# Attention and a feed-forward block in one kernel: one weight tile's sums kept in SBUF, and the order of GpSimd's work around them

## The chip, the cores and the metric

The kernel runs on one NeuronCore of a Trainium2 chip. The metric is the device time in microseconds of one execution, taken from the first to the last instruction with what lies around them; lower is better. The engines are named as the profile names them: PE (TensorE, matmuls; PEld are its weight loads), DVE (VectorE), ACT (ScalarE), POOL (GpSimd) and SP (SyncE, which issues the DMAs here).

## The reference

Masked attention over 8 batches, 8 heads, 576 positions and a head size of 64 (half of the heads look at a window of 32 positions, half at every 32nd position), and behind it a feed-forward block of 512 to 2048 to 512 over all 4608 tokens:

```python
scores = scale * np.matmul(q, k.transpose(0, 1, 3, 2))
scores = np.where(masks[None, :, :, :], scores, -1000000000.0)
scores = scores - np.max(scores, axis=-1, keepdims=True)
attn = np.exp(scores)
attn = attn / (np.sum(attn, axis=-1, keepdims=True) + 1e-09)
x = np.matmul(attn, v)          # heads side by side: 4608 x 512
h = x @ w_in                    # 512 x 2048
g = h * (1.0 / (1.0 + np.exp(-1.702 * h)))
out = g @ w_out                 # 2048 x 512
```

## The kernel before

Attention is worked in pairs (48 of them, six per batch, alternately of the windowed kind "l" with tiles of 96 rows and of the strided kind "s" with 128 rows). One pair passes through these steps: `scores` (PE, into the two banks `s_banks`), `masked` and `maxima` (DVE), `below` (subtract the maximum, GpSimd, but on DVE for pair 6, lines 301 to 304), `exps` (ACT), `totals` (DVE), `scaled` (GpSimd, line 323), `turn` (PE transposes, then an ACT copy `kept`), `values` (PE, again into `s_banks`) and the copies `moved` (ACT), which put the result into the four blocks x11, x12, x21, x22 of a batch's x.

The product with `w_in` is done batch by batch, over eight weight tiles (`FP` = 8). Every operand is split into a high part (a cast on ACT: `w_high`, `t_high`, `x_high`) and a low part (a subtraction on DVE: `w_low_part`, `t_low`, `x_low`), and three matmuls (high by high, high by low of x, low of w by high) stand for one. From the second batch on, and for tiles 6 and 7 of the first, the product of a weight tile is formed with seven block products instead of eight (`product(n, k)` and `combine(n, k)`, n counts tiles through all batches). These need sums and differences of the four blocks of x (`x_sum`, `first_sums`: s1 = x21 + x22, s2, s3 = x11 - x21, which is made in the place of x21, s4 = x12 - s2) and of the four blocks of each weight tile (`t_sum`, four GpSimd subtractions of 128x256, then `t_high` and `t_low` into kinds 3 to 6 of the tile). For tiles 0 to 5 of the first batch the eight plain block products are used (`plain(n, u)`, "units" of six matmuls), since their sums aren't there yet.

Where a tile's sums come from: the words of weight tile i arrive in a buffer `raw_i` and are decoded there by ACT and DVE (`w_scale`, `w_low`, `w_join`). For tiles in `DIRECT` (line 439: 0, 6 and 7) the sums are formed in that buffer, which then stays in use until `t_low`. The others are written to a DRAM tile (`w_store`, 512 KB) and read back later (`t_load`) into the shared tile `sums`, three at a time. Raw buffers, weight tiles `w_i`, `sums` and two early inputs rotate in nine buffers of the same size (`wp`, line 136).

The order of the work is written out by hand. The first pairs and the first unit are in `OPENING` (line 695). Then comes one slot after the other: a slot s issues one unit or product on PE, and behind it what `side(s, ...)` registered for it, in the order of registration (`sided`, line 1018). Slots 8 to 50 hold the units and the first products of tiles 6 and 7, pass 1 (batch 1, products n = 8 on) begins at slot 59 (`HEAD`). Every engine's instructions and every DMA issue stay in this program order (class `InOrder`, line 80), so an instruction that waits holds all that stands behind it on its engine. The slots of pairs 6 to 11 are set in lines 767 to 777, those of the raw words in 782 to 790, of the tiles' sums in 791 to 804, of the first batch's sums and differences in 805 to 809, and of later batches' x sums in 753 to 764.

Of the kernel before, what the change touches and what calls it, by code (L numbers as in the profile page):

```python
# [15 lines left out]
ALU = mybir.AluOpType  # L16
# [14 lines left out]
FP = DFF // (2 * P)  # L31
PAIRS = 6
# [10 lines left out]
PLAIN = 6  # L43
SEVEN = 8 * PLAIN - 3
# [28 lines left out]
def attn_ffn(ctx, tc, qk, vs, weights, masks, ident, out):  # L73
# [6 lines left out]
    class InOrder:  # L80
# [16 lines left out]
    vector, scalar, gpsimd, sync = (  # L97
        InOrder(e, strict) for e in (nc.vector, nc.scalar, nc.gpsimd, nc.sync)
    )
# [64 lines left out]
    for j in (1, 2, 3, 0, 4, 5):  # L164
# [3 lines left out]
        t = prs[j].rearrange("p (i m) -> p i m", i=4)  # L168
# [76 lines left out]
    def parts_of(p, banks, at=0):  # L245

        nq, nk, _, mask = geom(p)
        pr = pr_of(p).rearrange("p (i m) -> p i m", i=4)[:, :, 1 : 1 + 2 * WL]
        pr = pr.rearrange("p i (j n) -> p i j n", j=2)
        heads = pr[:nq, :, :, :nk]  # L250
        srcs = banks and [
            bank[:nq, at : at + 4 * WL].rearrange("p (i n) -> p i n", i=4)[:, :, :nk]
            for bank in banks
        ]
        if p not in sums_of:
            sums_of[p] = [
                small.tile([P, 8], F32, tag=x, name=f"{x}_{p}") for x in ("nmax", "ssum", "rinv")
            ]
        return nq, nk, mask, pr, heads, srcs, sums_of[p]
# [4 lines left out]
    def each(t, nk):  # L264
        t = t.rearrange("p (i j) -> p i j", j=2)
        return t.unsqueeze(3).broadcast_to([t.shape[0], 4, 2, nk])
# [33 lines left out]

    def below(p, banks):
        nq, nk, _, _, heads, _, (nmax, _, _) = parts_of(p, banks)
        engine = vector if p == PAIRS else gpsimd
        engine.tensor_tensor(out=heads, in0=heads, in1=each(nmax[:nq], nk), op=ALU.add)

    def exps(p, banks):
# [60 lines left out]
    def moves_of(moves):  # L367
        for u in range(U):
            for move in moves:
                move(u)  # L370
# [22 lines left out]
    def x_from(k, b):  # L393
        if b is None and k in (1, 6):
            return apart[(PLAIN + (k == 6)) % 2]
        names = {0: "11", 2: "12", 5: "22", 6: "21"} if b == 0 else ("11", "11", "12", "s3", "s1", "22", "12")
        return halves[names[k]]
# [12 lines left out]
    def x_sum(k, b):  # L410
        x11, x12, x21, x22, s1 = (halves[x] for x in ("11", "12", "21", "22", "s1"))
        s2 = x_from(1, b)
        if k == 1:
            vector.tensor_tensor(out=s1, in0=x21, in1=x22, op=ALU.add)
        elif k == 2:
            vector.tensor_tensor(out=s2, in0=x22, in1=x21, op=ALU.subtract)
        elif k == 3:
            (vector if b == 1 else gpsimd).tensor_tensor(
                out=x21, in0=x11, in1=x21, op=ALU.subtract
            )  # L420
        else:
            (vector if b == 1 else gpsimd).tensor_tensor(
                out=x12, in0=x12, in1=s2, op=ALU.subtract
            )


    def first_sums(*which):

        x11, x12, x21, x22 = (halves[x] for x in ("11", "12", "21", "22"))
        s2, s3, s1, s4 = (x_from(k, None) for k in (1, 3, 4, 6))  # L430
        for k in which:
            o, x, y, op = {
                1: (s2, x22, s3, ALU.subtract), 6: (s4, x12, s2, ALU.subtract),
                4: (s1, x21, x22, ALU.add), 3: (s3, x11, x21, ALU.subtract),
            }[k]
            gpsimd.tensor_tensor(out=o, in0=x, in1=y, op=op)

    KINDS = (0, 5, 1, 6, 3, 4, 2)
    DIRECT = (0, *range(PLAIN, FP))

    def w_words(which, i, raw):

# [37 lines left out]
    def w_store(i):  # L480
        if i not in DIRECT:
            sync.dma_start(out=plains[i].rearrange("p (q n) -> p q n", q=4), in_=words[i])
# [8 lines left out]
    def t_view(i):  # L491

        if i in DIRECT:
            return spent[i].rearrange("p (q n) -> p q n", q=4)
        if "sums" not in made:
            made["sums"] = wp.tile([P, WLEN], F32, tag="w", name="sums", bufs=FP + 1)
        k = i % 3
        return made["sums"][:, k * 1024 : (k + 1) * 1024].rearrange("p (q n) -> p q n", q=4)
# [4 lines left out]
    def t_sum(i, m):  # L503

        b11, b21, b22, b12 = ((words[i] if i in DIRECT else t_view(i))[:, q] for q in range(4))
        t3, t4, t5, t6 = (t_view(i)[:, q] for q in range(4))
# [209 lines left out]
    def side(s, f, *a):  # L716
        sides.setdefault(s, []).append((f, a))

    def first(b):
        return HEAD + PASS * (b - 1) if b else 0  # L720
# [16 lines left out]
    def groups_of(b, slots):  # L737

        for g in range(3):
            q, s, then = b * PAIRS + 2 * g, slots[g] + 3 * (g > 0), slots[g + 1]  # L740
            side(s, both_scores, q)
            for i in range(2):
                s += 2 * i * (g == 0)
                side(s + i, masked, q + i, s_banks, 256 * i)
                for f, d in (
                    (maxima, 0), (below, 0), (exps, 4), (totals, 5),
                    (scaled, 5 + (i and g > 0)),
                ):
                    side(s + d + i, f, q + i, s_banks)
                side(then - (3 - (g > 0), 1)[i], turn, q + i, s_banks[i])  # L750
            side(then, both_values, q)

    for b in range(B):
        at = first(b)
        if b:
            c = {1: -2, 2: 1}.get(b, 0)
            side(at - 10 - c, x_sum, 1, b)
            side(at - 9 - c, x_sum, 3, b)
            for k in range(7):
                t = at + 2 * k - 6 + (k == 1)  # L760
                side(t, x_high, k, b)
                side(t + 1, x_low, k, b)
            side(at - 4, x_sum, 2, b)
            side(at, x_sum, 4, b)
        if 1 < b < B - 1:
            groups_of(b + 1, [at + t for t in (3, 16, 30, 44)])
        for i in range(PAIRS if b < 2 else 0):
            p = (b + 1) * PAIRS + i
            s = at - 3 * b + 7 * i + 2 * (not b)
            t = ((4, 5, 6, 11, 12) if b else (2, 3, 3, 11, 13)) if not i else (4, 5, 5, 10, 12) if i == PAIRS - 1 and not b else (5, 6, 7, 10, 12)  # L770
            side(s, scores, p, s_banks)
            side(s, load_qk, p + 2)
            for f, d in ((masked, 0), (maxima, 1), (below, 2), (exps, t[0]), (totals, t[1]), (scaled, t[2])):
                side(s + d, f, p, s_banks)
            side(s + t[3], turn, p, s_banks[0])
            side(s + t[4], lambda p=p: moves_of([values(p, s_banks)]))
            side(s + t[4], load_v, p + 2)
# [4 lines left out]
    for i in range(2, FP):  # L782
        at = 7 * (i - 2) + 6
# [6 lines left out]
            side(at + t, f, i)  # L790
    for i in range(FP):
        if i in DIRECT:
            at = 7 * (i - 2) + 6
            for m in range(4):
                side(at + 4 + m // 2 if i else 9, t_sum, i, m)
            for t, f in ((8, t_high), (9, t_low)) if i else ((16, t_high), (17, t_low)):
                side(at + t if i else t, f, i)
            continue
        load = -8 + i if i < 4 else 7 * i - 20
        sums, high, low = (1, 5, 6) if i == 1 else (7 * i - 10 + t for t in (0, 6, 8))  # L800
        for m in range(4):
            side(HEAD + sums + (2 if i > 1 and m > 1 else 0), t_sum, i, m)
        for t, f in ((load, t_load), (high, t_high), (low, t_low)):
            side(HEAD + t, f, i)
    side(1, first_sums, 4, 3)
    side(5, first_sums, 1, 6)
    for t, k in ((18, 3), (24, 1), (31, 4), (SEVEN + 2, 6)):
        side(t, x_high, k, None)
        side(t + 1, x_low, k, None)

# [70 lines left out]
    for h in range(12):  # L881
        at = last + STEP * (h // 2) + 16 + 3 * (h % 2)
# [126 lines left out]
    for i, n in enumerate((0, 1, 2, 3)):  # L1009
        at = last + (15, 23, 31, 45)[i]  # L1010
# [14 lines left out]
    for s in range(8, first(B)):  # L1025
        if s in units:
            plain(*divmod(units[s], 8))
        else:
            at = s - HEAD + PASS
            for n in (at // STEP, at // STEP - 1):  # L1030
                k, odd = divmod(at - STEP * n, 2)
# [151 lines left out]
```

## Time and profile before

| | us |
|---|---|
| three runs, median (lowest, highest) | 847.0 (846.14, 847.84) |
| the profiled execution, its own time | 847.13 |
| its span, first to last instruction | 845.3 |
| PE busy | 822.4 |
| DVE busy | 607.2 |
| POOL busy | 507.3 |
| ACT busy | 418.1 |

The span is the time in which instructions run; the time of an execution has some 1.8 us more around it. Busy times count an engine's own instructions without its waits. The mean granted clock of PE in this execution was 0.986 of full speed.

### The profile page before, as it was taken

The page shows a single profiled execution, that of the slowest core. Times are in us where ns is not written, and L with a number is a line of the kernel's source. Part 1 is how long each engine was busy: PE and PEld are TensorE (multiplying, and loading weights), DVE is VectorE, ACT ScalarE, POOL GpSimd, SP SyncE. Part 2 cuts the span into 40 slices and gives each one's busy share as a digit, 9 for nine tenths or more (in the row PEclk, how much of TensorE's full clock was granted, in tenths as well). Part 3 has the DMA queues.
Part 4 walks back from the last instruction along what each step waited for, and adds up shares of the span by engine and source line. Part 5 has one row for each costly group of instructions (what it writes and reads, how often), then busy time and mean ns, then how long its engine had stood idle before and what let it go on. Part 6 is the DMA issues. An engine that isn't in the chain of part 4 may idle for free.

```text
span 845.3 us, 22494 instructions
## 1 busy us (share of the span) xinstructions
PE 822.4 (97%) x9020; PEld 768.5 (91%) x9025; DVE 607.2 (72%) x1026; ACT 418.1 (49%) x646; POOL 507.3 (60%) x511
## 2 busy tenths in 40 slices
PE   7978989999999999999999999999999999999998
PEld 5868979999999999999999999889889889888898
DVE  5756777676866777768567886888777667677774
ACT  4657533343443444444346565555555555555550
POOL 4644276144333333433335539999999999999990
PEclk9979989999999999999999999999999999999999
DMA  9787556476676685766757974444444444444431
GB/s 344 287 304 249 180 163 206 147 240 222 209 240 229 204 275 183 249 226 203 245 190 258 299 244 129 147 125 131 141 129 134 153 145 144 127 146 128 125 100 50
DMA packets 111640, 161.59 MB, mean 191 GB/s; under 512 B 9648, under 2 KB 88240, under 8 KB 110640
## 3 DMA queue, kind: packets, MB, share of 16 engines
q1 hardware_dynamic: 111536, 160.16, 58.3%
q8 instruction: 71, 1.16, 0.6%
q14 instruction: 33, 0.27, 0.1%
HBM read 102.97 MB, written 57.15 MB: 189 GB/s over the span
## 4 chain that ended last, share of the span: by engine, by line
PE 86%; DVE 0%; issue 0%
PE my L89 27%; PE mx L89 23%; PE mz L89 21%; PE s L89 15%; DVE w L89 0%; DVE arena L89 0%; DVE nmax L89 0%
## 5 line engine op out<-in xcount | busy, mean ns | idle before, releaser
L89 POOL TENSOR_TENSOR arena<-arena 128x256 f32<-128x256 f32 (+1 forms) x302 | 342.9, 1151 | 119.8 <-ACT arena L89 44.8
L89 DVE TENSOR_TENSOR xa<-arena,xa 128x576 fp32r<-128x576 f32 (+3 forms) x116 | 158.8, 1371 | 38.5 <-ACT xa L89 37.5
L89 PE MATMUL my<-xa,w 128*128 128x288 f32 x1128 | 180.8, 302 | 2.5 <-DVE w L89 2.5
L89 ACT CAST xa<-arena 128x576 fp32r<-128x576 f32 (+3 forms) x107 | 118.0, 1122 | 99.7 <-PE s L89 24.4
L89 PEld LDWEIGHTS my<-xa,w 128*128 128x128 f32 x1128 | 157.0, 189 | 5.3 <-DVE w L89 2.7
L89 DVE TENSOR_TENSOR arena<-my,arena 128x288 f32<-128x288 f32 (+1 forms) x230 | 100.3, 442 | 63.2 <-PE my L89 60.7
L89 ACT COPY arena<-mx 128x288 f32<-128x288 f32 (+3 forms) x167 | 57.6, 366 | 171.9 <-PE mx L89 112.0
L89 PE MATMUL mx<-xa,w 128*128 128x288 f32 x804 | 133.5, 304 | 3.8 <-ACT arena L89 3.8
L89 PE MATMUL mz<-xa,w 128*128 128x288 f32 x792 | 129.2, 299 | 0.5 <-DVE xa L89 0.5
L89 ACT ACTIVATE arena<-arena 128x1024 f32<-128x1024 f32 (+2 forms) x120 | 105.1, 876 | 36.3 <-POOL arena L89 20.9
L89 POOL TENSOR_TENSOR arena<-arena,nmax 96x512 f32<-96x512 f32 (+1 forms) x41 | 52.7, 1286 | 115.9 <-DVE nmax L89 108.3
L89 PEld LDWEIGHTS mx<-xa,w 128*128 128x128 f32 x804 | 116.6, 194 | 4.9 <-ACT arena L89 4.0
L89 PEld LDWEIGHTS mz<-xa,w 128*128 128x128 f32 x792 | 112.1, 189 | 1.4 <-DVE xa L89 0.7
L89 DVE TENSOR_TENSOR arena<-mz,arena 128x288 f32<-128x288 f32 (+1 forms) x172 | 75.2, 440 | 31.7 <-PE mz L89 27.6
L89 POOL TENSOR_TENSOR arena<-arena,rinv 96x512 f32<-96x512 f32 (+1 forms) x48 | 47.0, 988 | 54.9 <-DVE rinv L89 38.8
L89 PE MATMUL mx<-w_out,xa 128*128 128x512 f32 (+1 forms) x378 | 72.3, 317 | 0.0
L89 PE MATMUL mz<-w_out,xa 128*128 128x512 f32 (+1 forms) x366 | 71.4, 320 | 0.0
L89 PE MATMUL my<-w_out,xa 128*128 128x512 f32 (+1 forms) x366 | 71.3, 320 | 0.0
L89 DVE TENSOR_TENSOR ga<-arena,ga 128x1792 fp32r<-128x1792 f32 (+1 forms) x31 | 56.6, 1824 | 16.1 <-ACT ga L89 16.1
L89 PE MATMUL s<-w_out,xa 128*128 128x512 f32 (+1 forms) x378 | 67.8, 321 | 0.0
L89 ACT CAST ga<-arena 128x1792 fp32r<-128x1792 f32 (+1 forms) x25 | 40.8, 1632 | 46.6 <-PE s L89 10.4
L89 PEld LDWEIGHTS s<-w_out,xa 128*128 128x128 f32 x378 | 54.9, 188 | 5.8
(83 smaller groups left out, 1094.7 us busy)
## 6 DMA issues: line engine op xcount, KB each, us to landing
hid<-arena SPq DMA_DIRECT2D x256, 144.0 KB, 3.4
arena<-hid SPq DMA_DIRECT2D x144, 256.0 KB, 3.3
arena<-qk SPq DMA_DIRECT2D x23, 448.0 KB, 4.9
arena<-qk SPq DMA_DIRECT2D x21, 472.0 KB, 5.6
arena<-vs SPq DMA_DIRECT2D x23, 384.0 KB, 4.8
out<-arena SPq DMA_DIRECT2D x34, 256.0 KB, 3.9
stage<-w_out SPq DMA_DIRECT2D x16, 512.0 KB, 4.3
raw<-w_in SPq DMA_DIRECT2D x7, 1024.0 KB, 7.9
```

The lines of the kernel that those rows point to most:

```text
L89: ins = call(*args, **kw)
```

## The change

`below` of pair 7 goes from GpSimd to VectorE, like that of pair 6. Pair 6's transposes and value products come one slot earlier. For batch 1, `x_sum` 3 and 4 go from VectorE to GpSimd, where they are for all other batches. In `first_sums`, s2 is formed as s1 - x11 instead of x22 - s3 (the same value), so the order becomes s1, s2, s4, s3. Tile 1 joins `DIRECT`: its store and its load fall away, its sums are formed in its raw buffer in slots 19 and 20 (before: in slot 60), its casts are in slots 24 and 25 (before: 64 and 65). The casts of difference 1 of the first batch go from slots 24 and 25 to 27 and 28. Tile 0's casts, and sums and casts of tiles 6 and 7, come one slot later (38, 39, 42, 43 become 39, 40, 43, 44; 45, 46, 49, 50 become 46, 47, 50, 51). The loads of tiles 2 and 3 come one slot earlier.

```diff
@@ below
-        engine = vector if p == PAIRS else gpsimd
+        engine = vector if PAIRS <= p < PAIRS + 2 else gpsimd
@@ x_sum
-            (vector if b == 1 else gpsimd).tensor_tensor(
+            gpsimd.tensor_tensor(
                 out=x21, in0=x11, in1=x21, op=ALU.subtract
             )
         else:
-            (vector if b == 1 else gpsimd).tensor_tensor(
+            gpsimd.tensor_tensor(
                 out=x12, in0=x12, in1=s2, op=ALU.subtract
             )
@@ first_sums
-                1: (s2, x22, s3, ALU.subtract), 6: (s4, x12, s2, ALU.subtract),
+                1: (s2, s1, x11, ALU.subtract), 6: (s4, x12, s2, ALU.subtract),
@@
-    DIRECT = (0, *range(PLAIN, FP))
+    DIRECT = (0, 1, *range(PLAIN, FP))
@@ slots of pair 6: exps, totals, scaled, turn, values
-            t = ((4, 5, 6, 11, 12) if b else (2, 3, 3, 11, 13)) if not i else ...
+            t = ((4, 5, 6, 11, 12) if b else (2, 3, 3, 10, 12)) if not i else ...
@@
         if i in DIRECT:
-            at = 7 * (i - 2) + 6
+            at = 7 * (i - 2) + 11
+            places = ((9, 9, 17, 18), (19, 20, 24, 25))[i] if i < 2 else (at, at + 1, at + 4, at + 5)
             for m in range(4):
-                side(at + 4 + m // 2 if i else 9, t_sum, i, m)
-            for t, f in ((8, t_high), (9, t_low)) if i else ((16, t_high), (17, t_low)):
-                side(at + t if i else t, f, i)
+                side(places[m // 2], t_sum, i, m)
+            side(places[2], t_high, i)
+            side(places[3], t_low, i)
             continue
-        load = -8 + i if i < 4 else 7 * i - 20
-        sums, high, low = (1, 5, 6) if i == 1 else (7 * i - 10 + t for t in (0, 6, 8))
+        load = -9 + i if i < 4 else 7 * i - 20
+        sums, high, low = (7 * i - 10 + t for t in (0, 6, 8))
@@
-    side(1, first_sums, 4, 3)
-    side(5, first_sums, 1, 6)
-    for t, k in ((18, 3), (24, 1), (31, 4), (SEVEN + 2, 6)):
+    side(1, first_sums, 4, 1)
+    side(5, first_sums, 6, 3)
+    for t, k in ((18, 3), (27, 1), (31, 4), (SEVEN + 2, 6)):
```

## Rows read from the trace of the kernel before

**Rows 1.** The page, part 1: busy time, share of the span, instructions by engine
```profile
PE 822.4 (97%) x9020; PEld 768.5 (91%) x9025; DVE 607.2 (72%) x1026; ACT 418.1 (49%) x646; POOL 507.3 (60%) x511
```

**Rows 2.** Waits of PE from 30 us on: total us, times, longest us
```profile
PE s L89 <- ACT arena L89: 6.6, 2, 6.2
PE mx L89 <- ACT arena L89: 3.8, 1, 3.8
PE my L89 <- DVE w L89: 2.5, 1, 2.5
```

**Rows 3.** Windows: stretch, length, busy us by engine, granted clock, DMA share, GB/s
```profile
49.30:54.90 5.60, 5.60 (x51) 5.48 (x52) 3.45 (x5) 2.13 (x5) 2.39 (x2) 0.53 0.69 235
54.90:81.80 26.90, 26.89 (x449) 25.10 (x447) 20.12 (x32) 19.11 (x34) 9.76 (x11) 1.00 0.82 278
...
85.60:88.70 3.10, 3.10 (x13) 3.10 (x14) 2.04 (x2) 0.00 (x0) 0.93 (x2) 0.50 0.14 48
...
113.50:119.40 5.90, 5.90 (x64) 5.24 (x68) 2.66 (x6) 2.49 (x7) 3.26 (x4) 0.50 0.55 183
```

**Rows 4.** Timeline, POOL: start us, us, instruction, [idle before <-releaser]
```profile
34.22 3.18 POOL L89 TENSOR_TENSOR arena<-arena 128x576 f32<-128x576 f32 x2
37.77 0.92 POOL L89 TENSOR_TENSOR arena<-arena,rinv 128x432 f32<-128x432 f32 x1 [0.37 <-DVE rinv L89]
38.64 4.78 POOL L89 TENSOR_TENSOR arena<-arena 128x576 f32<-128x576 f32 x2
43.38 2.89 POOL L89 TENSOR_TENSOR raw<-raw 128x256 f32<-128x256 f32 x4
46.23 1.04 POOL L89 TENSOR_TENSOR arena<-arena,nmax 96x512 f32<-96x512 f32 x1
```

**Rows 5.** Timeline, ACT then PE, around the first wait
```profile
42.29 0.40 ACT L89 COPY arena<-mx 128x288 f32<-128x288 f32 x1
47.30 0.63 ACT L89 ACTIVATE arena<-arena 96x512 f32<-96x512 f32 x1 [4.61 <-POOL arena L89]
...
48.84 0.68 ACT L89 COPY arena<-s 128x108 f32<-128x108 f32 x4
...
49.27 1.41 PE L89 MATMUL s<-arena 64*64 64x54 f32 x32 [6.21 <-ACT arena L89]
...
54.86 0.49 PE L89 MATMUL s<-ident_sb,arena 96*128 96x96 f32 x4
```

**Rows 6.** Timeline, DVE: `below` of pair 6, tile 2's low part
```profile
34.73 1.37 DVE L89 TENSOR_TENSOR arena<-arena,nmax 128x432 f32<-128x432 f32 x1
...
40.88 1.27 DVE L89 TENSOR_TENSOR w<-raw,w 128x1024 fp32r<-128x1024 f32 x1 [0.16 <-ACT w L89]
```

**Rows 7.** Timeline, DVE, POOL and ACT, ahead of the second wait
```profile
77.50 0.67 DVE L89 TENSOR_REDUCE nmax<-arena 96x8 f32<-96x512 f32 x1
...
79.04 1.75 POOL L89 TENSOR_TENSOR arena<-arena,nmax 96x512 f32<-96x512 f32 x1
...
80.83 0.63 ACT L89 ACTIVATE arena<-arena 96x512 f32<-96x512 f32 x1 [1.59 <-POOL arena L89]
...
84.17 1.07 ACT L89 CAST w<-raw 128x1024 fp32r<-128x1024 f32 x1
85.11 0.43 ACT L89 COPY arena<-mx 128x288 f32<-128x288 f32 x1
```

**Rows 8.** Timeline, POOL, PE and DVE, around the third wait
```profile
103.36 4.47 POOL L89 TENSOR_TENSOR sums<-sums 128x256 f32<-128x256 f32 x4
...
109.37 0.93 PE L89 MATMUL mz<-xa,w 128*128 128x288 f32 x5 [0.47 <-DVE xa L89]
...
112.21 1.21 DVE L89 TENSOR_TENSOR w<-sums,w 128x1024 fp32r<-128x1024 f32 x1
```

**Rows 9.** Timeline, ACT and PE: tile 7's cast, products 7.1 and 6.5
```profile
93.64 1.06 ACT L89 CAST w<-raw 128x1024 fp32r<-128x1024 f32 x1
...
96.38 1.74 PE L89 MATMUL my<-xa,w 128*128 128x288 f32 x12
```

More of the change, by code (lines that the diff above doesn't have):

```diff
@@ L769, in attn_ffn @@
             s = at - 3 * b + 7 * i + 2 * (not b)
-            t = ((4, 5, 6, 11, 12) if b else (2, 3, 3, 11, 13)) if not i else (4, 5, 5, 10, 12) if i == PAIRS - 1 and not b else (5, 6, 7, 10, 12)
+            t = ((4, 5, 6, 11, 12) if b else (2, 3, 3, 10, 12)) if not i else (4, 5, 5, 10, 12) if i == PAIRS - 1 and not b else (5, 6, 7, 10, 12)
             side(s, scores, p, s_banks)
```

## The prediction

> **What bounds the kernel now.** I read the page's busy times first: TensorE (PE) is busy 822.4 of 845.3 us, so all its idle time is 22.9 us, and a change that leaves the matmuls alone can win that much and what the clock adds, no more [rows 1]. Then I read the waits of PE from 30 us to the end. Three matter: 6.2 us on ScalarE (ACT) before the score products, 3.8 us on ACT before a product in mx, 2.5 us on VectorE (DVE) for a weight tile [rows 2]; a fourth of 0.47 us stands in the timeline [rows 8]. After each long wait the windows show the clock at 0.50 to 0.53, that is 1.2 GHz instead of 2.4, for 5.6, 3.1 and 5.9 us of PE work [rows 3]. So each wait is paid twice. All lie between 43 and 120 us; the edits lie there or up to 10 us before.
>
> The first wait, read back from PE: the scores of pair 8 started at 49.27 after 6.21 us idle. They write the banks that the copies of pair 6's values empty, and these ran on ACT at 48.84, behind the exponentials of pair 7 at 47.30, for which ACT had idled 4.61 us [rows 5]. The exponentials waited for `below` of pair 7 on GpSimd (POOL) at 46.23, which stood behind four x sums of 128x576 and the four sums of weight tile 0; from 34.22 to 47.27 POOL had one gap of 0.37 us [rows 4]. So POOL's queue order is the bound there, through ACT.
>
> The second wait, the same way: unit 5.4 needs the copy of unit 5.3 at 85.11, behind tile 6's high part at 84.17, behind the exponentials of pair 11 at 80.83, which had waited 1.59 us for `below` at 79.04, itself behind two sums of tile 6 [rows 7]. The third: product 9.1 needs tile 1's low part, made at 112.21 from sums that stood at pass 1's start, 4.47 us on POOL [rows 8].
>
> **The change, first wait.** `below` of pair 7 leaves POOL (1.04 us) for DVE, behind the maxima there; DVE's row for pair 6 took 1.37 us beside POOL [rows 4, 6]. It can start near 40.8 and end at 41.5 to 42.2, four microseconds before POOL's 47.27. The copies of pair 6's values also move ahead of the exponentials on ACT (slots 12 and 14 instead of 13 and 15). ACT's copy at 42.29 ended at 42.69, four value copies take 0.68, so the banks are free near 43.4 at the latest, not 49.27 [rows 5]. The transposes of pair 6, one unit earlier, now wait some 0.75 us for POOL's scaling, which ends at 38.69 [rows 4]; from there three units of 0.8 and the value products' 0.66 bring PE to unit 2.0 at 42.2, and to the scores at 43.0 if nothing else waits.
>
> Two things become late next. (1) The low part of tile 2 stands on DVE behind the new `below`. It ran at 40.88 for 1.27 [rows 6]. Now it starts at 41.5 if DVE goes on at once, or at 42.7 if a POOL sum comes between, and ends at 42.7 to 44.0. Unit 2.0's third matmul would read it at 42.5: 0.2 to 1.5 us, I take 0.9, so the scores start near 43.9. (2) Scaling of pair 7 on POOL still stands behind tile 0's four sums, which ended at 46.23 [rows 4]. At 0.72 each they were undisturbed then; with DVE at work beside them they end at 46.3 to 48, the scaling (1.04) at 47.3 to 49, I take 48.3. PE is there at 43.9 + 0.66 for the scores + three units at some 0.8 (twelve matmuls in 1.74 [rows 9]) = 47.0. It waits 1.3 us (0.3 to 2), and the transposes of pair 7, which ran at 54.86 [rows 5], run near 48.4 (47.4 to 49.4). **Gain 6.4 us (5.4 to 7.5)**, the half clock of 49.3 to 54.9 included.
>
> The swap in `first_sums` (s2 as s1 - x11, made ahead of s3) keeps four POOL instructions of the same size: nothing by itself.
>
> **Tile 1.** Its four sums move to slots 19 and 20 on POOL: at 0.72 each [rows 4], 2.9 us, up to 4.5 beside a busy DVE [rows 8]. They need be done before slot 24, some 4 us later, and stand ahead of the scaling of pair 8, which has a unit or two to spare. Its high part (1.05 on ACT) and low part (1.21 on DVE) move to slots 24 and 25, where the casts of difference 1 stood; those go to 27 and 28. Cover: from 54.9 to 81.8 ACT was busy 19.11 of 26.9 us, DVE 20.12, POOL 9.76, and PE never waited [rows 3]. I cost them at nothing; without that cover they cost at most their 2.3 us. One store and one load of 512 KB go from SP's queue, with nothing waiting behind them. Tile 1's raw buffer is now held until slot 25, where two new tiles (w_4, raw_7) want buffers and one is free by my count of the nine. If SP's load waits, nothing behind it is pressing; if ACT's cast waits, up to 2 us. I take nothing and keep 2 for the range.
>
> **Second wait.** With tile 6's sums one slot later, `below` of pair 11 starts when its maxima are done (77.50 + 0.67, near 78.1), 0.9 us earlier, and takes 1.04 to 1.75 [rows 4, 7]. The exponentials then start at 79.2 to 79.9. From them to tile 6's cast ACT takes 84.17 - 80.83 = 3.34 us; that cast now stands behind the copy, so the copy starts at 82.6 to 83.2, and PE follows 0.48 later, at 83.1 to 83.7 instead of 85.6 [rows 3, 7]. The wait shrinks from 3.8 to 1.3 to 1.9 us. Taking 83.3: 2.3 us, and half of the 3.1 us at half clock, 1.55. **Gain 3.85 (3.4 to 4.05)** if the clock holds.
>
> **Tile 7** moves one slot too. Its cast ran at 93.64 for 1.06, and product 7.1 started at 96.38 [rows 9]. A slot (0.8) later, and with an x sum ahead of the subtraction, the low part is there near 97.3 instead of 96; the third matmul wants it at 96.65. **Loss 0.65 (0 to 0.9).**
>
> **Third wait.** Tile 1's low part is long done: the 2.47 us go, and nearly half of the 5.9 us at half clock, 2.8 [rows 2, 3, 8]. The 0.47 us for a difference's low part on DVE [rows 8] go too, since the two x sums of batch 1 and tile 1's subtraction (1.21) leave DVE there. On POOL the x sums cost 1.6 each [rows 4], where 4.47 us of tile 1's sums leave [rows 8]; what stands behind the second is the scaling of pair 12, with 2 us to spare. Next late would be tile 2's low part for product 10.1, which I find 2 us early. **Gain 5.7 (5.4 to 5.9).**
>
> **The sum.** 6.4 + 3.85 - 0.65 + 5.7 = 15.3 us. The profiled execution took 847.13 us (span 845.3), 0.13 above the median of 847.0. 847.13 - 15.3 = **831.8 us**. Low ends: 5.4 + 3.4 - 0.9 + 5.4 = 13.3, or 833.8. High ends: 17.45, or 829.7.
>
> **The rivals.** *The clock still drops at the waits that are left.* For: the remaining waits add up to 0.75 + 0.9 + 1.3 us near 39 to 48 and 1.5 us at unit 5.4, and after 2.5 us the clock fell [rows 2, 3]. Against: none is as long as 2.5 us. Price: half of 3 to 5 us at each, 1.5 to 2.5, two such: 831.8 + 4 = 835.8, and 839.6 with 2 us for the buffer and the low ends. *Nothing is left to wait for*: low part and scaling fit between, 6.2 + 3.8 + 2.5 + 0.5 + 2.4 + 1.55 + 2.8 = 19.7 us, 827.4. Against: POOL's queue in [rows 4] leaves no room for it. *The first wait has another end*: if the ACT queue, not `below`, holds the copies (the raw tiles' casts stand in it), 4 to 5 us of the first gain do not come: 841. Against: ACT idled 4.61 us ahead of just that instruction [rows 5].
>
> *GpSimd becomes the bound, and the kernel slower.* DVE's two-input instructions hold POOL up: two x sums took 4.78 us in one place and 3.18 in another [rows 4], and POOL now has tile 1's sums in slots 19 and 20 ahead of the scaling of pair 8. Its instructions from 34.22 to that scaling are some 16.4 us by the shorter rows (eight sums at 0.72, four x sums at 1.6, four pair steps near 1.05), and PE wants the result at about 55. At 1.16 times, as in the stretch 34.22 to 47.27 (11.2 us of such work in 13.05), it is there at 53.3, in time. At 2.2 times, 36 us, it is 15 us late and the gain is gone; at 2.5 times, 41 us, the end is some 852. No stretch of these rows is near that. The Trainium skill says of this (SBUF - State Buffer, "Who interferes with whom"): a VectorE instruction with two SBUF inputs contends with a GpSimd instruction that reads SBUF, and whichever issues second is blocked until the first finishes. The trace agrees: 4.78 against 3.18 us [rows 4]. By the rule alone, where every such VectorE instruction in slots 9 to 23 (an estimated 6 us) is added to POOL, the end would be some 4 us later, 836, still not slower.
>
> **How the numbers follow.** Forecast 0.58, clock 0.22, nothing left 0.08, another end 0.07, GpSimd the bound 0.05. The range 828.0 to 839.6 takes in the first two and part of the third. 0.2% (1.7 us) is about what a measurement of this kernel can tell from no change. Faster by more 0.92, within it 0.03, slower 0.05.
>
> **What would show it.** In the profile after: the wait of PE for ACT before the scores of pair 8 under 1 us, with a new one of about a microsecond before the transposes of pair 7, released by POOL's scaling; DVE's `below` near 41; the wait at unit 5.4 at 1.3 to 1.9 us; none for tile 1 at product 9.1, and a short one for tile 7 at 7.1; the clock full from 49 us on. Wrong: POOL behind PE at pair 8, a cast of tile 4 waiting for a buffer, or half clock between 44 and 55 as before.

## The result

The changed kernel takes 834.65 us (median of four runs, 834.5 to 835.13) against 846.57 (845.64 to 847.84) of the kernel before, run beside it: a ratio of 0.9859, 95% interval 0.9842 to 0.9876, 11.9 us less. The forecast was 831.8 us, in a range of 828.0 to 839.6. The profiled execution took 834.66 us, its span is 832.5 (before: 845.3).

The page of the changed kernel, busy times and granted clock in 40 slices:

```profile
PE 817.7 (98%) x9020; PEld 762.7 (92%) x9025; DVE 611.1 (73%) x1025; ACT 418.3 (50%) x646; POOL 517.1 (62%) x512
...
PEclk9999999999999999999999999999999999999999
```

PE's busy time fell by 4.7 us with the same 9020 matmuls [rows 1]: the half clock behind the three waits is gone, less short stalls inside groups of matmuls, which count as busy. Its idle time fell from 22.9 to 14.8 us. The waits of PE from 30 us on, in the same view as [rows 2]:

```profile
PE s L89 <- POOL arena L89: 2.7, 2, 2.2
PE mx L89 <- ACT arena L89: 1.5, 1, 1.5
PE my L89 <- DVE w L89: 0.5, 1, 0.5
PE s L89 <- ACT arena L89: 0.2, 1, 0.2
PE mz L89 <- DVE xa L89: 0.2, 1, 0.2
PE my L89 <- DVE arena L89: 0.2, 1, 0.2
```

The 6.2 us on ACT before the scores of pair 8 are gone, and in their place stands a wait of 2.2 us on POOL. The 3.8 us before a product in mx are 1.5. The 2.5 us for a weight tile are 0.5, and that is another tile. Where they stand, in the timeline of PE (start us, us, instruction, idle before it and what ended it):

```profile
38.86 0.66 PE L89 MATMUL s<-ident_sb,arena 128*128 128x128 f32 x4 [0.58 <-POOL arena L89]
...
43.63 0.69 PE L89 MATMUL s<-arena 64*64 64x54 f32 x32
...
49.05 0.55 PE L89 MATMUL s<-ident_sb,arena 96*128 96x96 f32 x4 [2.17 <-POOL arena L89]
...
78.26 1.84 PE L89 MATMUL mx<-xa,w 128*128 128x288 f32 x12 [1.48 <-ACT arena L89]
...
80.73 1.31 PE L89 MATMUL my<-xa,w 128*128 128x288 f32 x6
...
88.95 1.58 PE L89 MATMUL my<-xa,w 128*128 128x288 f32 x10 [0.50 <-DVE w L89]
```

The transposes of the pairs make good posts to measure between, since they are the same four matmuls in every kernel and can be found in the timeline at once (38.86 and 49.05 are those of pairs 6 and 7). The opening, which differs by up to 2.4 us from one profiled execution to the next, and what comes after the edits fall out of such differences. In us, from one pair's transposes to another's:

| | 6 to 7 | 7 to 10 | 10 to 11 | 11 to 13 | 13 to 17 | 6 to 17 |
|---|---|---|---|---|---|---|
| before | 16.10 | 23.15 | 12.23 | 31.99 | 29.98 | 113.45 |
| after | 10.19 | 23.97 | 8.87 | 27.18 | 29.96 | 100.17 |
| difference | -5.91 | +0.82 | -3.36 | -4.81 | 0.0 | -13.28 |
| forecast | -6.4 | 0 | -3.85 | -5.05 | 0 | -15.3 |

Column 6 to 7 holds the first wait, 10 to 11 the second, 11 to 13 the third with product 7.1. Of the 13.28 us, 0.5 went in the opening and in the later passes, so that the spans differ by 12.8.

How the first wait was resolved is read from three engines. POOL (compare [rows 4]), then DVE, then ACT (compare [rows 5]):

```profile
38.76 5.38 POOL L89 TENSOR_TENSOR arena<-arena 128x576 f32<-128x576 f32 x2
44.11 3.90 POOL L89 TENSOR_TENSOR raw<-raw 128x256 f32<-128x256 f32 x4
47.96 1.04 POOL L89 TENSOR_TENSOR arena<-arena,rinv 96x512 f32<-96x512 f32 x1
...
40.76 0.96 DVE L89 TENSOR_TENSOR arena<-arena,nmax 96x512 f32<-96x512 f32 x1
41.64 1.21 DVE L89 TENSOR_TENSOR w<-raw,w 128x1024 fp32r<-128x1024 f32 x1
...
49.12 2.53 DVE L89 TENSOR_TENSOR w<-raw,w 128x1024 fp32r<-128x1024 f32 x1 [1.99 <-ACT w L89]
...
42.38 0.73 ACT L89 COPY arena<-s 128x108 f32<-128x108 f32 x4
42.94 0.64 ACT L89 ACTIVATE arena<-arena 96x512 f32<-96x512 f32 x1
...
51.68 1.05 ACT L89 CAST w<-raw 128x1024 fp32r<-128x1024 f32 x1 [1.35 <-DVE w L89]
```

`below` of pair 7 runs on DVE at 40.76, the low part of tile 2 goes on at once behind it, the copies of pair 6 are done at 43.1 and the scores start at 43.63. POOL now sets the next wait: two x sums took 5.38 us instead of 4.78, the four sums of tile 0 took 3.90 instead of 2.89, and the scaling of pair 7, at 47.96, releases the transposes. The last line of DVE and the last of ACT show what the forecast had costed at nothing: ACT's cast of weight tile 3 waited 1.35 us, until tile 0's subtraction on DVE (49.12) was done. That subtraction took 2.53 us; one of the same size took 1.21 at 41.64.

### The profile page after: what moved, and what is told of

It is laid out like the page before. It is cut to its first block, busy times and chain, and to the rows that moved or that the text cites. A ratio compares the mean times of both kernels' runs of the same rounds, so it can differ in the third digit from the quotient of the medians.

```text
span 832.5 us, 22488 instructions
## 1 busy us (share of the span) xinstructions
PE 817.7 (98%) x9020; PEld 762.7 (92%) x9025; DVE 611.1 (73%) x1025; ACT 418.3 (50%) x646; POOL 517.1 (62%) x512
## 4 chain that ended last, share of the span: by engine, by line
PE 87%; DVE 0%; issue 0%
PE my L89 27%; PE mx L89 23%; PE mz L89 22%; PE s L89 15%; DVE arena L89 0%; DVE nmax L89 0%
## 5 line engine op out<-in xcount | busy, mean ns | idle before, releaser
L89 POOL TENSOR_TENSOR arena<-arena 128x256 f32<-128x256 f32 (+1 forms) x304 | 349.7, 1166 | 121.7 <-ACT arena L89 42.9
L89 PE MATMUL mx<-xa,w 128*128 128x288 f32 x804 | 130.2, 299 | 1.5 <-ACT arena L89 1.5
L89 POOL TENSOR_TENSOR arena<-arena,nmax 128x432 f32<-128x432 f32 (+1 forms) x40 | 50.1, 1253 | 106.2 <-DVE nmax L89 102.9
L89 PEld LDWEIGHTS mx<-xa,w 128*128 128x128 f32 x804 | 113.5, 189 | 2.5 <-ACT arena L89 1.7
```

The lines of the kernel that those rows point to most:

```text
L89: ins = call(*args, **kw)
```

## The experiments

Each line's time is a median, with the median of the kernel before in runs beside it; the posts are those of the table above.

| | us | before | 6 to 7 | 7 to 10 | 10 to 11 | 11 to 13 | 6 to 17 |
|---|---|---|---|---|---|---|---|
| only_below | 841.03 | 846.88 | 10.19 | 23.20 | 12.37 | 30.91 | 106.68 |
| no_below | 837.4 | 846.88 | 11.41 | 25.69 | 8.87 | 27.20 | 103.14 |
| tile1_dram | 836.81 | 846.88 | 10.18 | 23.21 | 8.88 | 28.98 | 101.35 |
| tiles67_early | 838.35 | 846.88 | 10.19 | 23.95 | 12.86 | 26.56 | 103.52 |
| fill_before | 845.06 | 846.96 | 13.94 | 23.15 | 12.38 | 32.24 | 111.69 |
| xsums_dve | 834.6 | 846.96 | 10.19 | 24.67 | 8.87 | 26.91 | 100.61 |
| s3_late | 834.98 | 846.96 | 8.82 | 25.27 | 8.87 | 27.18 | 100.12 |
| load6_late | 835.83 | 846.35 | 10.20 | 23.67 | 10.06 | 27.18 | 101.08 |
| s3_load6 | 834.24 | 846.35 | 8.83 | 25.05 | 10.06 | 27.19 | 101.10 |
| tile1_and_xsums | 838.85 | 846.35 | 10.20 | 26.07 | 8.88 | 31.54 | 106.66 |
| shifted | 833.62 | 846.35 | 8.82 | 25.04 | 7.99 | 27.38 | 99.20 |
| sums1_later | 835.69 | 846.16 | 8.84 | 24.50 | 10.55 | 27.04 | 100.89 |

What was expected of each run, and its rival, stand with the run.

**Which edit took the first wait?** One run makes that edit alone, one undoes it.

```diff
@@ only_below: the kernel before, one line changed
-        engine = vector if p == PAIRS else gpsimd
+        engine = vector if PAIRS <= p < PAIRS + 2 else gpsimd
@@ no_below: the changed kernel, the same line back
```

> The kernel before with one edit: `below` of pair 7 on VectorE; pair 6's copies stay behind pair 7's exponentials on ScalarE. My theory (GpSimd's queue holds `below`, and through it ScalarE): the exponentials of pair 7 run near 43 instead of 47.3, the copies of pair 6 near 44.5, the wait before the scores of pair 8 falls from 6.2 to about 1.5 us, and a new wait of 1 to 2 us stands before the transposes of pair 7, which come at 49 as in the changed kernel; the second and third waits stay with their half clock. About 841 us. Rival (ScalarE's own queue holds the copies, so only moving them helps): the wait stays near 6 us and the time near 846.5.

> The changed kernel with `below` of pair 7 back on GpSimd; pair 6's copies stay ahead of the exponentials. My theory: the scores of pair 8 no longer wait for it (the copies are ahead of the exponentials), so the wait moves: `below` at 47 to 48, the scaling of pair 7 at 50 to 51, and 3.5 to 5 us of idle before the transposes of pair 7, probably with half clock behind it. 837 to 839 us. Rival (the moved copies alone did the work): 834.7, as the changed kernel.

The edit alone gave 841.03 us, ratio 0.9936 (0.9916 to 0.9956). PE's timeline of it:

```profile
43.12 0.80 PE L89 MATMUL mz<-xa,w 128*128 128x288 f32 x4 [0.27 <-DVE w L89]
44.89 0.97 PE L89 MATMUL s<-arena 64*64 64x54 f32 x32 [0.97 <-ACT arena L89]
49.27 0.55 PE L89 MATMUL s<-ident_sb,arena 96*128 96x96 f32 x4 [0.84 <-POOL arena L89]
80.03 2.60 PE L89 MATMUL mx<-xa,w 128*128 128x288 f32 x12 [3.79 <-ACT arena L89]
...
108.08 1.28 PE L89 MATMUL my<-xa,w 128*128 128x288 f32 x4 [2.46 <-DVE w L89]
```

From pair 6 to pair 7 it takes the same 10.19 us as the whole change: at this place neither the earlier copies nor the new order in `first_sums` add anything, since POOL's scaling is late next in both. Second and third wait are untouched. So the place of `below` in POOL's queue alone is enough to account for the first wait. Undone, the edit costs 2.75 us against the changed kernel, not 5.9: with pair 6's copies ahead of the exponentials the scores don't wait for `below`, and the wait goes to the transposes of pairs 7 and 8:

```profile
49.66 0.55 PE L89 MATMUL s<-ident_sb,arena 96*128 96x96 f32 x4 [2.60 <-POOL arena L89]
54.75 0.93 PE L89 MATMUL s<-arena 64*32 64x64 f32 x48 [0.32 <-ACT arena L89]
59.91 0.66 PE L89 MATMUL s<-ident_sb,arena 128*128 128x128 f32 x4 [1.67 <-POOL arena L89]
```

So ACT's order had a part in it too: with `below` left on POOL the rest of the change still brings pairs 6 to 7 from 16.10 to 11.41 us, though pairs 7 to 10 then take 1.7 us longer than in the changed kernel. Either edit frees the scores; only `below` on DVE shortens POOL's queue. The earlier copies were not run by themselves.

**Is a wait paid twice?** The kernel before, with its first wait filled by 44 matmuls of 288 columns into a free bank, whose results nobody reads (code shortened).

```diff
+    def keep_busy():
...
+        for _ in range(44):
+            matmul(
+                six[4][:, :HALF], lhsT=w[:, 0, 0, 0], rhs=xv[0][:, 0, 0], start=True, stop=True,
...
+    side(16, keep_busy)
```

> The kernel before with 44 matmuls of 288 columns, whose results nothing reads, ahead of the scores of pair 8: they fill the first wait and change nothing else. My theory (each long wait is paid twice, once as idle time and once at half clock): PE busy through the wait, the granted clock stays full from 44 to 55, and the kernel is 2 to 2.6 us faster than before, 844.2 us. Rival (the slow matmuls after a wait are not the clock's cost, or other engines would hold PE anyway): 846.6, no change.

845.06 us, ratio 0.9982 (0.9973 to 0.9992), and 13.94 instead of 16.10 us from pair 6 to pair 7.

```profile
43.70 6.03 PE L89 MATMUL my<-xa,w 128*128 128x288 f32 x44
50.14 0.97 PE L89 MATMUL s<-arena 64*64 64x54 f32 x32 [0.41 <-ACT arena L89]
```

PE idled 0.41 us before the scores, which still started when ACT let them, and the granted clock was 1.00 from 43 to 56 us. So 2.2 us of the first wait's price were the 1.2 GHz after it, with no other work changed; I had 2.4 from [rows 3].

**The second wait.** The sums and casts of tiles 6 and 7 one slot earlier, as before.

```diff
-            at = 7 * (i - 2) + 11
+            at = 7 * (i - 2) + 10
```

> The changed kernel with the sums and casts of tiles 6 and 7 one slot earlier, as before. My theory: the wait at unit 5.4 goes from 1.5 back to 3.5 to 3.8 us with half clock behind it, the waits at products 6.1 and 7.1 (0.3 and 0.8 us) go: 836.5 to 837.5 us. Rival (the second wait shrank because pair 11 and its exponentials came earlier against PE for other reasons): 834, as the two short waits go.

838.35 us, 3.7 more than the changed kernel, and the old wait is back; the short wait at product 7.1 goes (11 to 13: 26.56 instead of 27.18):

```profile
80.84 3.25 PE L89 MATMUL mx<-xa,w 128*128 128x288 f32 x12 [3.78 <-ACT arena L89]
```

One slot for the sums and casts of these two tiles is worth 3.4 us from pair 6 to pair 17, above the 1.9 to 2.9 expected: behind the wait PE worked 4.6 us at half clock here, 3.1 before. The run moves the sums on POOL and the casts on ACT together. ACT's timeline of the changed kernel tells them apart (compare [rows 7]: exponentials of pair 11, copy of unit 5.3, tile 6's cast):

```profile
74.41 0.63 ACT L89 ACTIVATE arena<-arena 96x512 f32<-96x512 f32 x1 [0.17 <-POOL arena L89]
...
77.83 0.38 ACT L89 COPY arena<-mx 128x288 f32<-128x288 f32 x1
78.11 1.05 ACT L89 CAST w<-raw 128x1024 fp32r<-128x1024 f32 x1
```

Counted from the transposes of pair 10 (78.01 before, 73.02 after), the copy comes 2.3 us earlier. The exponentials already come 1.4 us earlier, because `below` no longer waits for sums on POOL; the other 0.9 us is the cast that now stands behind the copy.

**The third wait.** Tile 1 through DRAM again; the two x sums on DVE again; both.

```diff
@@ tile1_dram
-    DIRECT = (0, 1, *range(PLAIN, FP))
+    DIRECT = (0, *range(PLAIN, FP))
-        sums, high, low = (7 * i - 10 + t for t in (0, 6, 8))
+        sums, high, low = (1, 5, 6) if i == 1 else (7 * i - 10 + t for t in (0, 6, 8))
@@ xsums_dve, for k == 3 and k == 4
-            gpsimd.tensor_tensor(
+            (vector if b == 1 else gpsimd).tensor_tensor(
```

> The changed kernel with tile 1's sums through DRAM again, formed at pass 1's start. My theory: the third wait (2.5 us at product 9.1) and half clock behind it come back, 5.0 to 5.7 us, less up to 0.75 us that tile 1's work costs in slots 19 to 43: 839 to 840 us. Rival (the two x sums that left VectorE removed the third wait, by bringing the subtractions forward): 835.

> The changed kernel with x sums 3 and 4 of batch 1 back on VectorE. My theory: a cover, worth little: the wait for a difference's low part at product 8.4 goes from 0.2 back to about 0.5 us, the wait at product 7.1 stays; 835 us. Rival (the x sums are what gave the third gain): 838 or more.

Neither alone brought the wait back. Tile 1 cost 2.2 us (836.81), 1.8 of it between pairs 11 and 13, and the x sums nothing (834.6). For tile 1 alone 4 to 5 us were expected, so both were undone together:

> The changed kernel with two parts undone together: tile 1's sums through DRAM, and the x sums of batch 1 on VectorE. Each alone cost 2.2 and 0 us. Theory (either of them takes enough from VectorE ahead of product 9.1 to let tile 1's subtraction come nearly in time, so their gains overlap): the wait of 2.5 us at product 9.1 and the half clock behind it come back: 839 to 840 us. Rival (the parts add): 836.8.

838.85 us. Not all of that is the third wait: the profile also has PE at half clock for 7 us behind the wait at pair 7, and pairs 7 to 10 take 26.07 us where tile1_dram takes 23.21. The posts from 11 to 13 keep the two apart. The waits there in the timeline of PE, tile 1 alone undone and then both:

```profile
104.05 0.65 PE L89 MATMUL s<-ident_sb,arena 128*128 128x128 f32 x4 [1.66 <-POOL arena L89]
105.37 0.79 PE L89 MATMUL my<-xa,w 128*128 128x288 f32 x4 [0.40 <-DVE w L89]
```

```profile
102.80 0.93 PE L89 MATMUL mz<-xa,w 128*128 128x288 f32 x5 [0.47 <-DVE xa L89]
106.90 0.81 PE L89 MATMUL my<-xa,w 128*128 128x288 f32 x4 [2.48 <-DVE w L89]
```

With both undone the old waits of 0.47 and 2.48 us stand there again, and 11 to 13 takes 31.54 us against 31.99 before. With tile 1 alone undone the wait stands in two parts, 1.66 us for POOL's queue with x sum, tile 1's sums and scaling in it, and 0.40 for tile 1's low part. That is 0.9 us less idle time, and the granted clock stays at 1.00 behind it, where with both undone PE works some 3.4 us at half clock. So tile 1 alone brings the whole third gain (26.91 us with the x sums back on DVE), and the x sums alone would have brought 2.6 us of it, most of that by the clock. The two gains overlap: the single prices (1.8 and -0.3 us) don't add up to the 4.4 us that both together cost.

**What is left of the first wait.** If POOL's queue is all, then taking one x sum out from ahead of the scaling must win its time.

```diff
@@ s3_late: the changed kernel
-    side(5, first_sums, 6, 3)
+    side(5, first_sums, 6)
+    side(16, first_sums, 3)
```

> The changed kernel with s3 of the first batch taken out from ahead of tile 0's sums on GpSimd and put behind the scaling of pair 7. My theory (what is left of the first wait, 2.2 us before the transposes of pair 7, is GpSimd's queue, and so are the short waits for ScalarE behind it): the scaling of pair 7 ends 2 to 2.7 us earlier, the wait is under 0.3 us, and the kernel 2 to 2.7 us faster than the changed one, 832.3 us. Rival (something else is late next at the same place, the exponentials or the totals of pair 7): 834 to 834.7.

834.98 us: nothing. The wait before the transposes of pair 7 did fall, from 2.17 to 0.78 us, but pair 8 came no earlier (8.82 + 9.65 us from pair 6 to 8, where the changed kernel has 10.19 + 8.34). The timelines of POOL, DVE and ACT say why:

```profile
47.45 1.40 POOL L89 TENSOR_TENSOR arena<-arena 128x576 f32<-128x576 f32 x1
48.81 0.91 POOL L89 TENSOR_TENSOR arena<-arena,nmax 128x432 f32<-128x432 f32 x1
49.68 5.29 POOL L89 TENSOR_TENSOR raw<-raw 128x256 f32<-128x256 f32 x4
...
47.02 4.46 DVE L89 TENSOR_TENSOR w<-raw,w 128x1024 fp32r<-128x1024 f32 x1
...
51.52 1.05 ACT L89 CAST w<-raw 128x1024 fp32r<-128x1024 f32 x1 [1.59 <-DVE w L89]
```

Tile 0's subtraction began two microseconds earlier than in the changed kernel and ended at the same moment, after 4.46 us; meanwhile POOL's x sum and `below` ran at full pace. The cast of tile 3 waits for it, because it writes the buffer that tile 0's words leave: with tile 1's words held until slot 25 all nine buffers are, by my count, in use in slot 19. My theory for this place, POOL's queue alone, fell. The new one has two parts: buffers, and DVE's subtraction held up while POOL works. The first was tried by letting tile 3 have the free buffer:

```diff
@@ load6_late: the changed kernel; s3_load6: s3_late
-            side(max(0, 7 * (i - 3) - 3), load_w, i)
+            side(22 if i == 6 else max(0, 7 * (i - 3) - 3), load_w, i)
```

> The changed kernel with one number changed: the load of raw tile 6 is issued four slots later (22 instead of 18), so that weight tile 3 finds a free buffer in slot 19 and its cast on ScalarE need not wait for tile 0's subtraction on VectorE, which GpSimd's reads hold up. Theory of the buffers: ScalarE's wait of 1.4 us before that cast goes, the short waits of TensorE for ScalarE behind it (0.24 us and a few tenths) go, the wait before the transposes of pair 7 stays at 2.2 us: 0.5 to 0.8 us faster than the changed kernel, 834.0 us. Rival (only GpSimd's queue counts there): 834.6.

> s3 behind the scaling of pair 7, as in the run that brought nothing, and the load of raw tile 6 four slots later as well. Theory of the buffers (s3's move brought nothing because the cast of tile 3 waited for a buffer until tile 0's subtraction, 4.5 us long on VectorE, was done): now the 0.8 us at pair 7 stay, the 1.2 and 0.3 us behind it go, and the kernel is 1.5 to 2.5 us faster than the changed one, 832.5 us. Rival (another wait in the same place, the words of tile 3 or GpSimd itself): 834.6.

The cast no longer waits (ACT's timeline of load6_late):

```profile
49.88 0.48 ACT L89 COPY arena<-s 128x384 f32<-128x384 f32 x1
50.25 1.06 ACT L89 CAST w<-raw 128x1024 fp32r<-128x1024 f32 x1
```

and pairs 7 to 10 take 23.67 instead of 23.97 us, against 23.21 with tile 1 through DRAM. With s3 moved as well they take 25.05 instead of 25.27; the wait goes to DVE, whose subtraction is still 4.48 us long. So the buffer was real but worth only 0.2 to 0.3 us on balance. From pair 7 to pair 8 load6_late takes 7.84 us, as tile1_dram does, where the changed kernel takes 8.34; behind pair 8 it gives 0.2 us back. As whole kernels the two show no gain, 835.83 and 834.24 us; in both profiles the clock fell after the wait of 1.5 us at unit 5.4, which it had not done in the changed kernel. Windows around that wait (length, busy us of PE, PEld, DVE, ACT and POOL, clock, DMA share, GB/s), changed kernel and then load6_late:

```profile
75.70:78.20 2.50, 1.09 (x14) 0.82 (x6) 1.23 (x4) 2.50 (x9) 2.42 (x4) 1.00 0.28 89
78.20:81.00 2.80, 2.74 (x20) 2.67 (x20) 2.80 (x2) 1.36 (x3) 1.64 (x2) 1.00 0.50 147
```

```profile
75.70:78.20 2.50, 1.02 (x7) 0.79 (x7) 1.22 (x3) 2.50 (x9) 2.42 (x4) 1.00 0.22 68
78.20:81.00 2.80, 2.80 (x13) 2.80 (x13) 2.74 (x2) 0.71 (x1) 1.64 (x2) 0.53 0.51 146
```

The second part, with three more moves at the second wait (shifted) and then tile 1's sums behind the scaling of pair 8 (sums1_later):

```diff
@@ shifted: s3_load6, w_low of tile 7 two slots later, t_low of tile 6 one earlier, x_sum 1 of batch 1 one later
+        side(at + 1 - early[1] + 2 * (i == 7), word, w_low, i)
+            side(places[3] - (i == 6), t_low, i)
+            side(at - 10 - c + (b == 1), x_sum, 1, b)
@@ sums1_later: shifted, and
+            places = ((9, 9, 17, 18), (23, 25, 29, 30))[i] if i < 2 else (at, at + 1, at + 4, at + 5)
+            side({6: 22, 7: 28}.get(i, max(0, 7 * (i - 3) - 3)), load_w, i)
```

> s3 behind pair 7's scaling, the load of raw tile 6 later, and three moves at the second wait: tile 7's low words on ScalarE go behind the copy of unit 5.3 and tile 6's cast (slot 44 instead of 42), tile 6's subtraction one slot earlier and so ahead of tile 7's join on VectorE, the first x sum of batch 1 one slot later and so behind tile 7's subtraction. The wait at unit 5.4 goes from 1.5 to about 0.5 us, the waits at 6.1 and 7.1 (0.3 and 0.8) shrink or stay: 1 to 1.8 us faster than the run with s3 and the load alone, 831 us. Rival (the waits go to product 6.1 or to tile 7): no faster than that run.

> The run with the three moves at the second wait, and tile 1's four sums taken out of GpSimd's queue between slots 19 and 20 and put behind the scaling of pair 8 and behind `below` of pair 9 (slots 23 and 25; its casts in 29 and 30, the load of raw tile 7 in 28). Theory of the shared access to SBUF: tile 0's subtraction on VectorE (1.2 us alone, 4.5 us in the runs with s3 moved) is held up by GpSimd's unbroken queue there; with a gap in the queue it takes 2.7 us or less, the tile 3 subtraction behind it 1.2 instead of 1.75, and the transposes of pair 8 come 1 to 1.5 us earlier against those of pair 6 (16.5 to 17 us instead of 17.9). 832.5 us. Rival (the subtraction waits for something else, its cast or its buffer): unchanged there, 833.6.

The first is the fastest kernel of all, 833.62 us (833.19 to 834.04), ratio 0.9849 (0.9832 to 0.9865); the interval overlaps that of the changed kernel, and between the posts it is 1.0 us shorter. The wait at unit 5.4 fell to 0.49. The second shows what holds up the long subtraction (timelines of DVE and POOL):

```profile
46.73 2.91 DVE L89 TENSOR_TENSOR w<-raw,w 128x1024 fp32r<-128x1024 f32 x1
...
50.95 1.21 DVE L89 TENSOR_TENSOR w<-raw,w 128x1024 fp32r<-128x1024 f32 x1
...
48.52 1.89 POOL L89 TENSOR_TENSOR arena<-arena,nmax 128x432 f32<-128x432 f32 x1
53.60 0.92 POOL L89 TENSOR_TENSOR arena<-arena,rinv 128x432 f32<-128x432 f32 x1 [3.18 <-DVE rinv L89]
```

With tile 1's sums moved away from behind `below` of pair 8 it takes 2.91 us instead of 4.47, the next one 1.21 instead of 1.75, and pairs 6 to 8 take 17.04 us instead of 17.94, a little short of what was expected. So POOL's queue sets the length of this subtraction. It was not the pause itself that let it in, since that begins at 50.4 us and the subtraction ended at 49.6: here it went ahead of `below`, which took 1.89 us instead of 0.91. By what rule the two engines take turns is not shown. As a kernel it lost, 835.69 us: tile 1's words are held longer still, and later the cast of tile 6 on ACT had no buffer until a store of raw words had landed:

```profile
74.26 0.83 ACT L89 CAST w<-raw 128x768 fp32r<-128x768 f32 x1 [3.49 <-DMA plains<-raw]
```

## Why the prediction was right

It named the bound, the three waits and what would be late behind each, and missed by 2.9 us.

**The first wait** was read rightly back to `below` in POOL's queue; only_below shows that this alone is enough. Of the two things forecast as late next, the low part of tile 2 was not: DVE went on at once, and it came within the lower of the two cases (0.2 us, where I took 0.9). The scaling of pair 7 was late and ended at 49.0, the top of the 47.3 to 49 given, where I took 48.3; PE stood there at 46.9, forecast 47.0, so the wait was 2.17 us and over the 0.3 to 2. The gain was 5.9 us instead of 6.4.

**Tile 1 at no cost** is the step that failed. I read the cover from busy shares of a stretch, where ACT, DVE and POOL each had room [rows 3]. The posts show 0.82 us more from pair 7 to pair 10, and nothing of it with tile 1 through DRAM (23.21 against 23.15 before). I had counted the nine buffers and seen the tight place in slot 25; the one that bit was slot 19, for tile 3. That is 0.5 us between pairs 7 and 8, and load6_late shows it. The rest lies behind pair 8; that it comes from DVE's subtractions, longer beside POOL's four more sums, is likely but not shown by a run of its own.

**The second wait**: 1.48 us, forecast 1.5. The gain was 3.36 instead of 3.85, since product 6.1 then stood for tile 6's low part for some 0.3 us, which I had not priced.

**Product 7.1** waited 0.50 us and took 0.78 us longer than before in all, forecast 0.65. **The third gain**: 4.81 us from pair 11 to pair 13 where the forecast had 5.05 with that loss in it. The size was right, and so was giving it to tile 1: with the x sums back on DVE all of it stays. The 0.47 us, which I gave in part to the x sums, went without them. What I had not seen is that the x sums alone would have brought 2.6 us, which is why undoing tile 1 alone cost less than expected.

**The sum**: 15.3 forecast, 13.28 between the posts, 12.8 in the span, 11.9 between the medians. Of the last difference, 0.56 us is that the profiled execution of before, against which I summed, lay that much over the median of its four runs.

**The rivals.** The clock stayed full in the changed kernel's profile from 25 us on, so that rival didn't come about there; its condition was nearer than I thought, since in four other profiles the clock fell after waits of the same length. GpSimd as the bound of the whole stage didn't come about (two x sums grew by 1.13 times, tile 0's four sums by 1.35, and tile 1's took 5.30 us at 49.84, 1.8 times the 2.89; none 2.2 times). The rule of the Trainium skill on VectorE and GpSimd (SBUF — State Buffer, "Who interferes with whom") gave 836 by adding every such instruction to POOL; the end came out between that and my sum. No run here isolates what the rule alone would cost. That a VectorE subtraction of 1.21 us took 4.46 beside GpSimd's work agrees with it in kind. In one point it does not: by the rule the later of two waits for the earlier, and here the subtraction of s3_late, begun at 47.02, let three GpSimd instructions go first that began after it.

Not settled: why the later passes took up to 2.3 us more or less from one profiled execution to another, which hides differences under some 0.2%. The new order in `first_sums`, the earlier copies of pair 6 and the moved casts of difference 1 were not run by themselves.

## What to carry to other kernels

Where engines work through fixed queues, follow a wait back to the instruction that stands in the wrong queue, and price the edit by who is late next, not by the idle time that goes. Undo parts one at a time and then together: two edits whose gains overlap look cheap one by one. And a busy share is no cover: count the buffers slot by slot, and where two engines lengthen each other's instructions, as VectorE and GpSimd did here, add their work up.

## What the hardware showed

- The same wait did and did not bring the clock down. After the 1.5 us at unit 5.4 it fell to 1.2 GHz in two of eight profiles that have this wait (load6_late, s3_load6), after the 2.2 us at pair 7 in two of six (xsums_dve, tile1_and_xsums). After 2.6 us at pair 7 (no_below) it stayed full, while after 2.46 to 2.48 us at product 9.1 it fell in all four profiles that have that wait. The fall cost 1.2 us at unit 5.4 (10 to 11: 10.06 against 8.87), and 0.7 and 2.9 us at pair 7 (7 to 10: 24.67 against 23.97, 26.07 against 23.21).
- A VectorE subtraction of 128x1024 with both inputs in SBUF took 1.21 us at its shortest and up to 4.5 us beside GpSimd's work (2.53 in the changed kernel, 2.91 in sums1_later, 4.46 in s3_late). In s3_late it let an x sum, `below` and the first of tile 1's sums go by at their full pace before it ended: it lost against several instructions in a row, not one.
- It holds both ways: four GpSimd sums of 128x256 took 2.89 us with VectorE idle (before, 43.38) and 3.6 to 5.3 us beside it (changed kernel).
